# Three feature tiles of a projection abreast on the first chunk of tokens, weights and some last stores on ScalarE's queue, and a planner fed with traced transfer times

## The chip, the cores and the metric

The kernel runs on one core of one Trainium2 chip. Time is the device time of one execution in microseconds (us). Before the change it is 802.28 us, the median of three runs (800.56 to 803.45). A profiled execution gives the trace from which all durations here are read. The engines are PE (TensorE, matmuls; PEld is its weight load), ACT (ScalarE), DVE (VectorE), POOL (GpSimd) and SP (SyncE, which here issues nearly all transfers).

## The reference

Two independent branches over 2048 tokens of 448 features are computed, and their results stand side by side in an output of 2048 x 896.

```python
# A: Fourier mixing, y = Re(DFT_seq(DFT_hidden(x)))
a = einsum("bsd,ed->bse", x, dft_hid_re)
b = einsum("bsd,ed->bse", x, dft_hid_im)
y = einsum("ts,bse->bte", dft_seq_re, a) - einsum("ts,bse->bte", dft_seq_im, b)
# B: softmax attention, 16 heads of 28 features
q, k, v = split(x @ wqkv)
p = softmax(q @ k.T * 28 ** -0.5)
o = (p @ v).reshape(B, S, D) @ wo
# result
concatenate([y, o], axis=-1)
```

## The kernel before

**Products.** Most products are made of rounded high parts and small remainders: x = xh + xl, w = wh + wl, and xh wh + xl wh + xh wl is summed. A contraction over 448 features is three tiles of 128 and one of 64, whose high and low rows share one tile; so one product of a 128 x 512 block takes 11 matmuls: three for each of the first three tiles of features (quarters, below) and two for the last. ACT copies a landed piece into its rounded high part, DVE subtracts to get the low part.

**Stages.** Tokens come in 4 chunks of 512 (`load_x`, four transfers of 256 KB per chunk, one for each quarter of the features). `project` makes q and k of one feature tile of 128 (7 tiles, weights by `Piece`, 256 KB each) for the chunks that it is given; `values` makes v for a chunk, in four tiles of 128 tokens. The results go to DRAM (`qkd`, `vd`). Then the Fourier branch's hidden product (`hidden_both`, L891), its sums over mirrored rows (`combine`) and its sequence product in 4 chunks for each of two parts (`sequence_halved`, L1175) run between the attention of 16 heads: score matmuls (L1434), their exponential on ACT (L1438), and value matmuls (L1445) in groups of 16 tiles. `normal` takes a head's row sums through DRAM and multiplies by their reciprocals; `project_late` multiplies by `wo` (L1676 for the first three quarters of the features, L1707 for the last, which needs the last heads).

**The planner.** Nothing of the order is written out by hand. `Schedule` collects every instruction as a task with its engine, an estimated duration, dependencies, the buffers that it takes and a key, which is the time at which it is due. `run` then plays the kernel through: each free engine takes the ready task with the least key, and that fixes the order of each engine's queue when the kernel is built. On the chip each queue runs in that order and waits where something isn't there. The durations and the transfer times in it are constants: `FLOW_IN` and `FLOW` for the rate of transfers, `FIRST` for when an engine begins, `PE_TURN` for the switch from score to value matmuls, and for each transfer a size and an `extra`. `T_ATT` and `T_END` spread the keys of the 16 heads, `T_FILL` spreads those of all other matmuls (the fill), `T_OUT` is the key of the last stage, and `PV_LATE` puts the key of a group of value matmuls so many steps (one score matmul's share of the time of attention) behind its last score.

**Buffers.** `kept` is a pool of 20 pairs of 128 x 512 values that nearly every stage uses; a group of value matmuls holds 8 of them. `whi` and `wraw` have 3 buffers each, `wlo` has 5. Of the 8 PSUM banks 4 belong to the fill, 4 to attention, which may borrow the fill's.

**The start.** PE runs 11 warm-up pairs on an identity matrix (L1535). SP issues x's first quarter, the weights of feature tile 0, x's other three quarters, then the weights of v. PE runs the 11 matmuls of feature tile 0 for chunk 0, in the order in which their pieces come, then the values of chunk 0, then tile 0 for chunks 1 to 3, then the values of chunks 1 to 3, then the feature tiles 1 to 6 for all four chunks.

**The end.** In `project_late` the first nine matmuls of an output tile run early. Of the 16 tiles, those from 0 to `N_HELD` - 1 are copied out and held in SBUF until the last quarter's two matmuls are added by DVE; the others stay in a fill bank, and the last two matmuls add to it. Each tile is stored by SP (L1712 for held ones, L1716 for the others). After that every engine loads a flag that says whether the shortcuts held (L1746) and branches past a slower way to compute the same (L1747).

Of the kernel before, what the change touches and what calls it, by code (L numbers as in the profile page):

```python
# [22 lines left out]
D = 448  # L23
H = 16
DH = 28
# [18 lines left out]
N_WARM = 11  # L44
GV = 4
# [6 lines left out]
N_HELD = 12  # L52
# [11 lines left out]
NOTE_AT = 7.0  # L64
# [7 lines left out]
PV_LATE = 8.0  # L72
LATE_BOTH = 3.0
LATE_SPREAD = 3.5
LATE_RAW = 1.0
LATE_FIRST = 1.05
LATE_SUMS = 1.1
# [98 lines left out]
class Schedule:  # L176
# [38 lines left out]
    def run(self):  # L215
# [10 lines left out]
        while True:  # L226
            for e in self.ENGINES:
# [115 lines left out]
def tile_kernel(ctx, tc, xa, wre, wim, wd, xb, wqkv, wo, out):  # L343
# [122 lines left out]
    def dma(key, emit, size=256, extra=0.0, n=1, **kw):  # L466

        return sch.add({"SP": 0.4}, key, lambda e: emit(), dmas=[(size, extra)] * n, **kw)
# [22 lines left out]
    T_END = 740.0  # L491
    T_FILL = 950.0
    T_OUT = 806.0
# [74 lines left out]
    def load_x(c, key):  # L568
        cols = slice(c * CH, (c + 1) * CH)
        for k in range(4):  # L570
            pair = kept_s.slot()
            raw = Half(pair, 0)
            ld = dma(key + 0.3 * k, lambda raw=raw, k=k: nc.sync.dma_start(raw.t, xb[c, :, k]), use=[pair])
# [11 lines left out]
    def load_w(w, src, key, after=(), early=False):  # L585
        ts = []
        for k in range(4):
            raw = kept_s.slot() if early else wraw.slot()
            r2 = lambda raw=raw: raw.t.rearrange("p a b -> p (a b)")[:, :D]
            ld = dma(key + 0.3 * k, lambda r2=r2, k=k: nc.sync.dma_start(r2(), src(k)), acq=[raw])  # L590
# [9 lines left out]
    class Piece:  # L600


        def __init__(self, src, key, kind="c", early=False):
            self.hi, self.lo = whi.slot(), wlo.slot()
            raw = wraw.slot()
            ld = dma(key, lambda: nc.sync.dma_start(raw.t, src()), acq=[raw])
# [42 lines left out]
    def project(j, w, chunks):  # L649

        for c in chunks:
# [4 lines left out]
            first = j == 0  # L656
# [10 lines left out]
            else:  # L667
# [6 lines left out]
            end = chain(key, seq, o, CH, [], [w.hi, w.lo], M512, own, parts)  # L674
            key, out_key = (0.0, 11.0) if first else (key - 10, key - 10)
# [5 lines left out]
                dma(out_key, lambda hi=hi, cols=cols: nc.sync.dma_start(f32(qk_d[j * P:(j + 1) * P, 0, cols]), as_f(hi.t)), deps=[a], use=own),  # L681
                dma(out_key, lambda lo=lo, cols=cols: nc.sync.dma_start(f32(qk_d[j * P:(j + 1) * P, 1, cols]), as_f(lo.t)), deps=[b], use=own)]
# [1125 lines left out]
```

## Time and profile before

| | us |
|---|---|
| median of three runs | 802.28 (800.56 to 803.45) |
| the profiled execution's own time | 803.39 |
| span in it, first to last instruction | 801.5 |
| PE / ACT / DVE / POOL busy | 785.5 / 589.1 / 422.1 / 66.4 |
| mean granted clock of TensorE | 0.992 |

In a row of the timeline stand the start, the length, the engine, the line, the operation, the tile written and those read, their shapes and how many instructions were merged; in brackets stands how long the engine was idle before it and what ended that. SPq is the queue of SP: its length there is the time of issue, not of the transfer. In the list of waits the arrow points to what was waited for. In the table of stages each engine has its busy time and, in brackets, its number of instructions. In the chain that ended last, each piece was released by the one ahead of it.

### The profile page before, as it was taken

How to read it: one execution, taken by the hardware profiler on the slowest of the kernel's cores; microseconds unless marked ns; L12 is line 12 of the kernel's file. 1: busy time of each engine (PE TensorE's matmuls, PEld its weight loads, DVE VectorE, ACT ScalarE, POOL GpSimd, SP SyncE). 2: the span in 40 equal slices, each digit the busy share in tenths (PEclk: the TensorE clock that was granted, in tenths of full speed). 3: DMA queues.
4: the chain of work that ended last, by engine and by line, in shares of the span. 5: the costliest groups of instructions: out<-in, count | busy, mean ns of one | idle time of the engine just before them, and what ended most of it. 6: DMA issues, size and time to landing. Idle time of an engine off the chain costs nothing.

```text
span 801.5 us, 14235 instructions
## 1 busy us (share of the span) xinstructions
PE 785.5 (98%) x4721; PEld 476.3 (59%) x4721; DVE 422.1 (53%) x894; ACT 589.1 (74%) x1218; POOL 66.4 (8%) x220
## 2 busy tenths in 40 slices
PE   8999999999999999999999999999999999999995
PEld 7886555665566556555555555565455555555584
DVE  6642234262253456225477665668877766664342
ACT  6106887747878588888888887888788788889831
POOL 3000000000001010100121110111021102100000
PEclk9999999999999999999999999999999999999998
DMA  8857856652467756475678874785787867875143
GB/s 284 250 148 251 228 179 183 196 199 100 129 159 176 220 173 189 140 211 159 192 237 241 270 233 134 232 276 173 184 269 215 249 179 242 255 242 175 27 127 112
DMA packets 148023, 157.09 MB, mean 196 GB/s; under 512 B 39832, under 2 KB 116214, under 8 KB 147942
## 3 DMA queue, kind: packets, MB, share of 16 engines
q1 hardware_dynamic: 144774, 152.41, 63.2%
q0 software_dynamic: 3168, 3.69, 1.6%
q8 instruction: 40, 0.66, 0.4%
q14 instruction: 41, 0.34, 0.1%
HBM read 114.59 MB, written 50.99 MB: 207 GB/s over the span
## 4 chain that ended last, share of the span: by engine, by line
PE 88%; DMA 4%; ACT 3%; DVE 2%; SPq 1%; issue 1%; POOL 0%; DVEq 0%; ACTq 0%; POOLq 0%
PE bank L1434 29%; PE bank L1445 27%; PE bank L636 13%; PE bank L1175 8%; PE bank L891 5%; ACT kept L1438 3%; PE bank L1676 3%; DMA edge<-wim 1%; PE bank L1707 1%; PE bank L1418 1%; DMA xraw<-wim 1%; DMA kept<-xb 1%; DMA wdraw<-wim 1%; DMA kept<-ond 1%; PE bank L1094 0%
## 5 line engine op out<-in xcount | busy, mean ns | idle before, releaser
L1438 ACT ACTIVATE kept<-bank 128x512 f32<-128x512 f32 x1024 | 509.7, 676 | 111.3 <-PE bank L1434 102.7
L1434 PE MATMUL bank<-q,k 85*128 85x512 f32 x1024 | 362.3, 424 | 0.3 <-DVE kept L1273 0.3
L1434 PEld LDWEIGHTS bank<-q,k 85*128 85x128 f32 x1024 | 184.6, 190 | 87.9 <-issue 33.1
L1445 PE MATMUL bank<-kept,v 128*32 128x512 f32 x2048 | 234.3, 598 | 0.0
L1445 PEld LDWEIGHTS bank<-kept,v 128*32 128x32 f32 x2048 | 60.2, 110 | 133.7 <-issue 130.4
L1175 PE MATMUL bank<-zt 128*128 128x226 bf16 x448 | 78.1, 266 | 1.2 <-DVE zt L1218 1.2
L487 DVE COPY kept<-bank 128x448 f32<-128x448 f32 (+3 forms) x66 | 32.1, 508 | 84.6 <-PE bank L891 52.4
L636 PE MATMUL bank<-xt,whi 128*128 128x512 f32 x196 | 70.1, 402 | 1.5 <-DVE xt L481 1.3
L1131 DVE TENSOR_REDUCE diff<-zt 128x1 f32<-128x512 bf16 x77 | 51.6, 679 | 2.2 <-POOL zt L1228 0.7
L1175 PEld LDWEIGHTS <-zt 128*128 128x128 bf16 x448 | 30.6, 99 | 35.4 <-issue 25.9
L636 PEld LDWEIGHTS bank<-xt,whi 128*128 128x128 f32 x196 | 36.7, 191 | 13.1 <-issue 2.5
L636 PE MATMUL bank<-xt,wlo 128*128 128x512 f32 x112 | 44.0, 394 | 0.0
L891 PE MATMUL bank<-wd,whi 128*128 128x450 f32 (+3 forms) x128 | 42.1, 379 | 0.0
L1175 PE MATMUL bank<-xt,whi 128*128 128x448 f32 (+1 forms) x128 | 40.1, 339 | 1.1 <-DVE kept L1273 1.1
L636 PE MATMUL bank<-wd,xt 128*128 128x448 f32 x176 | 37.1, 368 | 0.0
L636 PEld LDWEIGHTS bank<-wd,xt 128*128 128x128 f32 x176 | 32.8, 188 | 3.5 <-issue 0.7
L1218 DVE TENSOR_TENSOR zt<-wdraw,xraw 128x508 bf16<-128x508 f32 x28 | 19.1, 682 | 25.4 <-PE bank L1175 10.6
L1129 ACT ACTIVATE spent<-zt 128x512 uint8<-128x512 bf16 x35 | 25.1, 716 | 5.3 <-DVE zt L1209 3.0
L1421 DVE STREAM_TRANSPOSE kept<-bank 128x512 f32<-128x512 f32 (+1 forms) x20 | 14.2, 712 | 27.2 <-PE bank L1418 27.2
L1175 PEld LDWEIGHTS bank<-xt,whi 128*128 128x128 f32 x128 | 25.0, 201 | 5.7 <-ACT kept L1438 1.7
L487 DVE CAST wd<-bank 128x512 fp32r<-128x512 f32 x8 | 5.5, 690 | 43.2 <-PE bank L636 43.2
L1498 ACT ACTIVATE kept<-bank 128x512 f32<-128x512 f32 (+1 forms) x19 | 11.3, 595 | 22.9 <-PE bank L1445 21.3
(172 smaller groups left out, 722.4 us busy)
## 6 DMA issues: line engine op xcount, KB each, us to landing
wdraw<-wim SPq DMA_DIRECT2D x38, 256.0 KB
qkd<-wd SPq DMA_DIRECT2D x32, 256.0 KB
wdraw<-wre SPq DMA_DIRECT2D x32, 256.0 KB
q<-qkd SPq DMA_DIRECT2D x64, 112.0 KB
k<-qkd SPq DMA_DIRECT2D x64, 112.0 KB
abd<-kept SPq DMA_DIRECT2D x16, 448.0 KB
kept<-abd SPq DMA_DIRECT2D x16, 448.0 KB
qkd<-kept SPq DMA_DIRECT2D x24, 256.0 KB
```

What stands on the lines that cost most here:

```text
L487: nc.vector.tensor_copy(dst, src)
L636: nc.tensor.matmul(o.t[:, :cols], w(), x(), start=(i == 0), stop=(i == n - 1))
L891: nc.tensor.matmul(o.t[:, c0:c1], of(w, i), y(), start=n == 0, stop=n == m)
L1129: nc.scalar.activation(spent, src(), AF.Abs, accum_out=dst)
L1131: nc.vector.tensor_reduce(dst, src(), axis=AX.X, op=ALU.add, apply_absolute_value=True)
L1175: nc.tensor.matmul(o.t[:, at0:at0 + n], cut_of(w.t, e, c), x(), start=first, stop=stop)
L1218: e.tensor_tensor(turned(dl.t, 1, 1, P - 1), mirror(r.t), read(base.t, 1, 1, P - 1), op=minus)
L1421: r = dve(key, lambda o=o, mt=mt: nc.vector.transpose(mt.t[:32 * n, 0], o.t[:32 * n]), 0.64, deps=[m], acq=[mt], use=[o], own=RAW_S)
L1434: m = pe(key, lambda e: nc.tensor.matmul(b.t, KT[h][kt // 4].t[:KR + 1, kt % 4 * P:(kt % 4 + 1) * P], q.t[:KR + 1, :], start=True, stop=True),
L1438: return act(key - 20, lambda: nc.scalar.activation(p.t, b.t, AF.Exp, scale=SCALE), deps=[m], use=[b, pair])
L1445: nc.tensor.matmul(o.t[j * VW:(j + 1) * VW, :], VT[h].t[:, kt // 4, kt % 4, :], tiles[i // 2].t[:, i % 2, :], start=(kt < 4 // len(cs)), s ...
L1676: nc.tensor.matmul(o.t[:, :D], a(), b(), start=(i == 0), stop=(i == 8 and n < N_HELD))
```

## The change

Chunk 0 is projected for feature tiles 0, 1 and 2 before its values are made. The weights of these three tiles are issued by ScalarE's queue ahead of its own work, the chains of tiles 1 and 2 are not tied to the chain of tile 0, and each of their matmuls depends only on its own piece of x and w. Later the loop over tiles gives tiles 1 and 2 only chunks 1 to 3. There are 9 warm-up pairs instead of 11 and 10 held output tiles instead of 12. Of the tiles that are not held, those of odd number are stored by ScalarE's queue. All other edits are numbers of the planner: transfers get an issue time (`each`) and another `extra`, and the rates, the turn, the due times and `PV_LATE` change. `VALUES` replaces `GV` with the same groups of four.

```diff
-N_WARM = 11
-GV = 4
+N_WARM = 9
+EARLY = 3
+VALUES = (4, 4, 4, 4)
...
-N_HELD = 12
+N_HELD = 10
...
-NOTE_AT = 7.0
+NOTE_AT = 9.0
...
-PV_LATE = 8.0
-LATE_BOTH = 3.0
...
+PV_LATE = 11.0
...
-FLOW, FLOW_IN = 250.0, 400.0
+FLOW, FLOW_IN = 250.0, 260.0
...
-FIRST = {"PE": 1.4, "ACT": 2.0, "DVE": 2.0, "POOL": 5.0, "SP": 0.75}
-FLOW_AT = 4.1
+FIRST = {"PE": 1.4, "ACT": 0.75, "DVE": 2.0, "POOL": 5.0, "SP": 0.75}
+FLOW_AT = 2.4
...
-PE_TURN = 0.22
-GAP = 0.6
+PE_TURN = 0.33
+GAP = 0.3
 JOIN = 15.0
-LAG = 60.0
+LAG = 100.0
...
-                    for size, extra in t.dmas:
+                    for size, extra, each in t.dmas:
...
-                        landed.append(max(at + 1.9 + size / 100 + extra + (3.0 if T_IN - 6 < now < 42 else 0.0), flow + 1.1))
-                        at += 0.38
+                        landed.append(max(at + 1.9 + size / (100 if now > T_IN - 6 else 140) + extra + (3.0 if T_IN - 6 < now < 42 else 0.0), flow + 1.1))
+                        at += each
...
+    def dma_act(key, emit, lat, **kw):
+
+        return sch.add({"ACT": 0.42}, key, lambda e: emit(), lat=lat, own=lat, **kw)
...
-    T_END = 740.0
-    T_FILL = 950.0
-    T_OUT = 806.0
+    T_END = 720.0
+    T_FILL = 930.0
+    T_OUT = 815.0
...
-            ld = dma(key, lambda: nc.sync.dma_start(raw.t, src()), acq=[raw])
+            if early:
+                ld = dma_act(key - 5, lambda: nc.scalar.dma_start(raw.t, src()), 4.6, acq=[raw])
+            else:
+                ld = dma(key, lambda: nc.sync.dma_start(raw.t, src()), each=0.66, acq=[raw])
...
-    def project(j, w, chunks):
+    def project(j, w, chunks, last=last):
...
-            first = j == 0
+            first = j == 0 or j < EARLY and c == 0
...
-            end = chain(key, seq, o, CH, [], [w.hi, w.lo], M512, own, parts)
-            key, out_key = (0.0, 11.0) if first else (key - 10, key - 10)
+            end = chain(key, seq, o, CH, [], [w.hi, w.lo], M512, own, parts, last)
+            key, out_key = (0.0, 11.0 + j) if first else (key - 10, key - 10)
...
-        return Piece(lambda: wqkv[:, :, j * P:(j + 1) * P], 0.2 if j == 0 else key, "w", j == 0)
+        return Piece(lambda: wqkv[:, :, j * P:(j + 1) * P], 0.2 + 0.25 * j if j < EARLY else key, "w", j < EARLY)
...
-        return pe(key, emit, d=0.22 * len(kts) * len(cs), deps=[*es, *got_v[h], after], use=[*tiles, VT[h], o], mode=1)
+        return pe(key, emit, d=0.2133 * len(kts) * len(cs), deps=[*es, *got_v[h], after], use=[*tiles, VT[h], o], mode=1)
...
-        s2 = dma(key, lambda: nc.sync.dma_start(sm.t[:, :n * NC], osb.t[DH:n * VW:VW, :]), 8, 3.0, deps=[a], use=[sm, pair])
+        s2 = dma(key, lambda: nc.sync.dma_start(sm.t[:, :n * NC], osb.t[DH:n * VW:VW, :]), 8, 0.6, each=0.67, deps=[a], use=[sm, pair])
...
-    w_0 = weights_of(0)
+    w_early = [weights_of(j) for j in range(EARLY)]
...
-    project(0, w_0, [0])
+    for j in range(EARLY):
+        project(j, w_early[j], [0], last if j == 0 else [None])
     values(wv, [0])
-    project(0, w_0, [1, 2, 3])
+    project(0, w_early[0], [1, 2, 3])
     values(wv, [1, 2, 3])
     x_users.append(v_last[0])
     for j in range(1, 7):
-        project(j, weights_of(j), range(NC))
+        project(j, *((w_early[j], range(1, NC)) if j < EARLY else (weights_of(j), range(NC))))
...
-                dma(key, lambda pair=pair, n=n: nc.sync.dma_start(out[n * P:(n + 1) * P, D:], pair.t[:, 0, :D]), deps=[e], use=[pair])
+                if n % 2:
+                    dma_act(key, lambda pair=pair, n=n: nc.scalar.dma_start(out[n * P:(n + 1) * P, D:], pair.t[:, 0, :D]), 3.0, deps=[e], use=[pair])
+                else:
+                    dma(key, lambda pair=pair, n=n: nc.sync.dma_start(out[n * P:(n + 1) * P, D:], pair.t[:, 0, :D]), deps=[e], use=[pair])
```

More of the change, by code (lines that the diff above doesn't have):

```diff
@@ L939, in put @@
                                   rows_at(src, (P - p) * row if p else P, [[P * row, HT], [-row, r], [1, FT * P]]))
-            base_turned[part, n] = dma(key + n * step, put, 256 if n else 16, extra=4.0, hold=True)
+            base_turned[part, n] = dma(key + n * step, put, 256 if n else 16, extra=1.5, each=0.75, hold=True)
     def turn_rows():
@@ L1063, in put @@
                 nc.sync.dma_start(x.t[:65:32, 1, CH - 1:], rows_at(src, HT * P * row + FT * P, [[0, 3], [1, 1]]))
-        ld = dma(key, put, 12, n=3 - part, extra=6.0, deps=[*zs, ab_done[FT], ab_done[HT + FT], *after], use=[w, x])
+        ld = dma(key, put, 12, n=3 - part, extra=6.0, each=0.9, deps=[*zs, ab_done[FT], ab_done[HT + FT], *after], use=[w, x])
         wide = lambda p0=0: w.t.rearrange("p a b -> p (a b)")[p0:96, part::2]
@@ L1469, in head_once @@
             got_q.append([*load_q((h, c), q, at - 14), dma(
[L1470 removed]
+                at - 11, lambda q=q, row=row: nc.sync.dma_start(f32(q.t)[KR:KR + 1, :], row), size=2, extra=0.4, each=0.3, deps=[s], use=[q])])
             qs.append(q)
@@ L1485, in head_once @@
                 es.append(score(h, c, kt, qs[c], got_q[c], tiles[-1], i % 2, key))
-            last_pv = four(h, po, tiles, es, key + PV_LATE * DT, range(GV * g, GV * (g + 1)), range(NC), last_pv)
+            last_pv = four(h, po, tiles, es, key + PV_LATE * DT, range(first, first + n), range(NC), last_pv)
+            first += n
         normal([(h, c) for c in range(NC)], h, po, last_pv, key + 10)
```

74 lines of the change are left out of this document (35 added, 39 removed).

## The prediction

> **What bounds the kernel now.** I read the page's head and busy shares first, then the slices with the chain of waits, then PE's waits, and last a table of stages and the timelines of both ends.
>
> ```profile
> span 801.5 us, 14235 instructions
> PE 785.5 (98%) x4721; PEld 476.3 (59%) x4721; DVE 422.1 (53%) x894; ACT 589.1 (74%) x1218; POOL 66.4 (8%) x220
> PE   8999999999999999999999999999999999999995
> PEclk9999999999999999999999999999999999999998
> PE 88%; DMA 4%; ACT 3%; DVE 2%; SPq 1%; issue 1%; POOL 0%; DVEq 0%; ACTq 0%; POOLq 0%
> ```
>
> TensorE (PE) is busy 785.5 of 801.5 us, only the first and last slices are not full, and 88% of the chain that ends last is PE's. So only 16.0 us can be won without taking work from PE. The list of PE's waits and the stages say where they lie:
>
> ```profile
> PE bank L1418 <- ACT kept L1438: 1.5, 1, 1.5
> PE bank L1535 <- POOL ident masks.py:199: 1.4, 1, 1.4
> PE bank L636 <- DVE xt L481: 1.3, 1, 1.3
> PE bank L1175 <- DVE zt L1218: 1.2, 2, 0.8
> PE bank L1175 <- DVE kept L1273: 1.1, 1, 1.1
> PE bank L1707 <- DVE q L1697: 0.8, 1, 0.8
> ...
> 5.00:10.00 5.00, 4.30 (x16) 3.20 (x15) 2.89 (x6) 2.81 (x6) 1.52 (x15) 1.00 0.94 303
> 10.00:15.00 5.00, 4.40 (x21) 3.98 (x22) 4.88 (x9) 4.73 (x9) 1.24 (x12) 1.00 1.03 375
> 20.00:25.00 5.00, 5.00 (x24) 4.13 (x23) 4.88 (x11) 2.30 (x4) 0.00 (x0) 1.00 1.07 303
> 790.00:801.50 11.50, 2.47 (x11) 1.62 (x10) 1.94 (x3) 1.69 (x3) 0.00 (x0) 0.76 0.25 87
> ```
>
> A wait's columns are its total, how often, and the longest. Those of a stage its length, then PE, weight loads, DVE, ACT and POOL busy, the granted clock, the DMA share and GB/s. The last stage alone has 9.0 us without matmuls (11.50 - 2.47). The longest wait in the middle is 1.5 us; three (1.5, 1.2 and 1.1) make 3.8 us. So three places can change: the start, the end, and the order in between.
>
> **The start.** This is the first chunk of tokens before the change; the last row gives the pitch of a 512-column matmul.
>
> ```profile
> 0.76 1.28 ACT L575 ACT_TABLE_LOAD   x1 [0.76 <-PEq L1801]
> 0.76 0.39 SPq L573 DMA_DIRECT2D kept<-xb  x1
> 1.21 0.69 SPq L606 DMA_DIRECT2D wraw<-wqkv  x1
> 1.38 5.07 PE L1535 MATMUL bank<-ident 128*128 128x128 f32 x22 [1.38 <-POOL ident masks.py:199]
> 4.49 0.63 ACT L575 ACTIVATE xt<-kept 128x512 fp32r<-128x512 f32 x1 [2.44 <-DMA kept<-xb]
> 5.32 0.63 ACT L607 ACTIVATE whi<-wraw 128x512 fp32r<-128x512 f32 x1 [0.20 <-DMA wraw<-wqkv]
> 5.98 0.56 DVE L611 TENSOR_TENSOR wlo<-wraw,whi 128x384 fp32r<-128x384 f32 x1
> 6.10 1.62 PE L636 MATMUL bank<-xt,whi 128*128 128x512 f32 x3
> 6.46 0.28 DVE L620 TENSOR_TENSOR wlo<-wraw,whi 64x128 fp32r<-64x128 f32 x1
> 9.20 0.63 ACT L575 ACTIVATE xt<-kept 128x512 fp32r<-128x512 f32 x1 [1.18 <-DMA kept<-xb]
> 9.86 0.69 DVE L481 TENSOR_TENSOR xt<-kept,xt 64x512 fp32r<-64x512 f32 x1 [1.12 <-ACT xt L575]
> 11.18 0.77 PE L636 MATMUL bank<-wd,xt 128*128 128x448 f32 x3
> 60.43 7.75 PE bank L636 x34
> ```
>
> A matmul of 512 columns takes 7.75 / 34 = 0.228 us. The 11 of the first chain need 2.51 us, but from the first (6.10) to the start of the values (11.18) pass 5.08: 2.57 us are lost, because each quarter of x comes only as fast as its transfer, the last at 9.20. The change puts 22 more matmuls into these holes (feature tiles 1 and 2 of the same tokens, 5.02 us, taken out of later places). Before, the same 33 and their holes count as 11.18 + 5.02 = 16.20 on this clock. With no hole and the same start they end at 6.10 + 33 x 0.228 = 13.62: a gain of at most 2.6 us. It can't be had in full:
>
> - Two more weights must come, 256 KB each. At 303 GB/s (stage 5 to 10) 512 KB are 1.7 us of transfer. If all of it comes ahead of x, the first matmul is at 7.8 and the 33 end at 15.3: gain 0.9 us. If only the last quarter of x is late (10.9), it has its 0.63 on ACT and 0.69 on DVE by 12.3, the six matmuls that need it (1.37 us) end at 13.7, and almost nothing is lost.
> - ACT makes three weights instead of one, 7 x 0.63 = 4.4 us with x, from 4.49 on: done by 8.9 if nothing waits, and the last x comes later anyway. The three issues stand ahead of the table load, which carries the line of the first activation (L575); at 0.69 each (SP's row) they and the 1.28 us load end by 0.76 + 2.07 + 1.28 = 4.11, before the first x at 4.49. This cover is thin: were the load first, the first weight would be issued at 2.04 instead of 1.21 and all would start 0.8 us later.
> - DVE makes two more low halves (0.56 + 0.28 each, 1.7 us) in 5 to 10, where it is busy 2.89 of 5 us. From 10 on it has no room (4.88 of 5), but there it also gets these 1.7 us back, since the same work stood there later.
> - SP's queue loses the weight ahead of x's second quarter (0.69 us) and so issues x sooner. The four stores of the extra tiles (256 KB each) move to 11 to 16 us, between loads of later x, as key 11 + j puts them; PE needs that x 3 us later than before, which covers them.
> - Two warm-up pairs fewer (5.07 / 11 = 0.46 us each) end the warm-up at 5.5 instead of 6.45; matmuls wait for data at 6.1, so I cost this at nothing.
>
> I take **-1.7 us**, midway between 0.9 and 2.6; the bounds for the range are 0 (loads crowded and table load first, 0.9 - 0.8) and -2.6.
>
> The Trainium skill's page "DMA: Bandwidth & Descriptors", section "Issuing engines are not separate DMA queues", speaks against part of this: transfers issued from different engines share the same 16 DMA engines and interleave, and a second issuer saves only issue time. The stage 10 to 15 agrees as far as it goes (DMA share 1.03). By that rule the two weights are paid for in full, the start gives 0.9 instead of 1.7 us, and the sum is 798.8.
>
> **The end.**
>
> ```profile
> 780.00:790.00 10.00, 10.00 (x51) 9.28 (x50) 2.90 (x5) 1.06 (x3) 0.00 (x0) 1.00 0.38 125
> 780.29 1.78 PE L1707 MATMUL bank<-wout,q 128*128 128x448 f32 x8
> 791.38 1.88 PE L1707 MATMUL bank<-wout,q 128*128 128x448 f32 x8 [0.79 <-DVE q L1697]
> 792.66 2.90 SPq L1716 DMA_DIRECT2D out<-kept  x4
> 792.90 0.55 ACT L485 ACTIVATE kept<-bank 128x448 f32<-128x448 f32 x1 [0.27 <-PE bank L1707]
> 793.30 0.62 DVE L487 COPY kept<-bank 128x448 f32<-128x448 f32 x1 [0.18 <-PE bank L1707]
> ...
> L1746 SPq TENSOR_LOAD <-flag x1: 609/609/609, 795.6 to 795.6; - x1
> L1747 SPq COMPARE_BRANCH  x1: 50/50/50, 796.6 to 796.6; - x1
> SPq L1747 <- SPq L1747: 2.6, 1, 2.6
> L1747 DVEq EVENT_SEMAPHORE  x1: 21/21/21, 797.8 to 797.8; - x1
> ```
>
> The last copy is done at 793.92, but SP issues the four last stores one behind another until 795.56, then loads the flag, branches at 796.6, waits 2.6 us and only then (799.2) runs out to 801.5. DVE, which branched earlier, was through at 797.8. After the change tiles 13 and 15 (and 11, by `n % 2` from tile 10 on) go by ScalarE's queue. SP's last store then waits only for ACT's copy (793.45), takes some 0.5 us and ends near 794.0 instead of 795.56. ACT's last store starts at 793.92 and ends near 794.4. With the same way to the end behind it SP is through at 797.7, about where DVE is. So up to 1.6 us go; I take **-1.4 us**, bounds -1.7 and 0 (the landing of the last store, not the branch, would then set the end). On ACT a store waits for DVE's copy, and behind it stand only the next tile's copy and the flag: at worst one DVE copy, 0.6 us, included in the bound.
>
> With 10 held tiles, 6 stay in the four fill banks; tiles 14 and 15 can begin their 9 matmuls only when tiles 10 and 11 have left. Of the 51 matmuls between 780 and 790 (0.196 us each), 8 belong to chunk 2's rest; the other 43, or 8.4 us, are such work that had not run by then, more than the 18 x 0.196 = 3.5 us of tiles 14 and 15, so the wait for a bank is covered. If chunk 2's rest came less than 3.5 us before the fill ends, the difference would be lost; two additions on DVE go, off the path.
>
> **The order in between.** All other edits alter no instruction of the kernel but the planner's costs, due times and transfer times, so each queue's order changes over 800 us. Attention's due times close 20 us sooner (740 to 720) and the fill's too (950 to 930). The fill's due times run evenly from about 52 to 950, so (950 - 740) / 898 = 23.4% of it is due behind attention before and (930 - 720) / 878 = 23.9% after. That half per cent of the fill, itself less than half of PE's 785.5 us, is at most 2 us more cover for the last head's chain, where PE waited 0.8 us. No transfer stands among PE's waits, so truer landings have little to win; new order shifts the 3.8 us of middle waits about. Bounds: all 3.8 and the 0.8 gone, or as much again, +4.6. I take a quarter of the gain, **-1.2 us**, as nothing in the diff addresses those buffers by itself.
>
> **Sum.** The profiled execution took 803.39 us (span 801.5 and 1.9 around it): 803.4 - 1.7 - 1.4 - 1.2 = 799.1. It lies 1.1 above the median of 802.28, so I forecast 798.0 for a median.
>
> **Rivals** (0.3%, 2.4 us, is about what a measurement of this kernel can tell from no change: 799.9 and 804.7).
>
> 1. **The order loses too (slower).** The third edit of weight is that value groups come due 11 steps late instead of 8. A step is (740 - 35) / 1024 = 0.69 us before and 0.67 after, so a group's 8 buffer pairs of 20 are held 7.4 instead of 5.5 us. Where two groups and a sum's three buffers are wanted at once the pool is dry, and PE's fill waits for DVE's freeing as at L1273, 1.1 us. Against it: this wait came once in 801 us. It decides if it comes at all eight chunks of the sequence stage: + 8 x 1.1 - 1.7 - 1.4 = +5.7, about 808. Five such waits, +2.4, already make it slower. Chance 0.11.
> 2. **The loads are crowded, the end is held by landings (no change).** Start -0.9 by the sum above, end -0.3, middle 0: 801.1. For it: DMA share 1.03 in 10 to 15; against it: the last x quarter, not the first, is what PE waits longest for. Chance 0.25. (By the Trainium skill's rule above, the start goes this way.)
> 3. **The new order also removes the middle's waits.** -2.6 - 1.6 - 4.6 = -8.8 from the start's and end's bounds: about 793.5. Chance 0.14.
> 4. **It doesn't do what it says:** the extra chains stand in PE's fixed order where their weights aren't there yet, so PE waits as before in other places. Start 0, end -1.4, middle 0: 800.9. Part of "no change", within rival 2's chance.
>
> The forecast itself (796 to 799.9) has 0.50. Range 793.0 to 804.0: from rival 3 to the upper side of no change; left out are rival 1 and a little below. Faster 0.64 (forecast and rival 3), same 0.25, slower 0.11.
>
> **What would show it.** Start: three weight loads issued on ACT before 2.9 us, the table load behind them, 33 matmuls with x and whi or wlo before the first with wd, and that one near 14.5 (16.2 would be no gain). End: the span ends about 6 us after the last copy instead of 7.6, with SP's last store ending within 0.5 us of it. Middle: no wait in PE's list over 1.5 us. The forecast is wrong if the first matmul with x comes after 7.0, if a wait of PE on DVE's kept stands three times or more, or if the last group of matmuls waits over 2 us for its q.

## The result, and the profile after

The change makes the kernel slower: **805.48 us** (median of 22 runs, 802.05 to 810.48) against 801.55 us (22 runs, 796.73 to 806.83), ratio 1.0054 with a 95% interval of [1.0032, 1.0076]. The forecast was 798.0, with a range of 793.0 to 804.0. The profiled execution took 807.78 us.

The page of the kernel after, first its head and slices:

```profile
span 805.9 us, 14248 instructions
PE 790.5 (98%) x4717; PEld 476.8 (59%) x4717; DVE 424.0 (53%) x900; ACT 582.7 (72%) x1199; POOL 69.8 (9%) x220
PE   7999999999999999999999999999999999999997
PEclk9999999999999998999999999999989999999999
```

PE is busy 5.0 us longer (790.5 for 785.5) at the same work. Two slices of the granted clock show an 8 in the middle, where the kernel before has none. PE's waits after:

```profile
PE bank L1437 <- DVE kept L487: 3.4, 2, 2.1
PE bank L639 <- ACT whi L610: 3.3, 2, 2.9
PE bank L1540 <- POOL ident masks.py:199: 1.4, 1, 1.4
PE bank L1437 <- DMA q<-md: 0.7, 1, 0.7
```

With one of 0.2 us these are all, 9.0 us in sum where the list of before had 7.8. That doesn't make 4 us. The time shows in the table of stages, by its granted clock (the column ahead of the last two):

```profile
7.90:11.31 3.41, 2.99 (x6) 1.66 (x6) 2.31 (x6) 1.78 (x5) 0.00 (x0) 0.50 1.06 357
300.00:304.90 4.90, 2.81 (x14) 2.06 (x13) 2.04 (x6) 4.06 (x9) 0.53 (x2) 1.00 0.71 204
304.90:311.70 6.80, 6.80 (x28) 2.87 (x30) 1.49 (x4) 2.75 (x6) 0.00 (x0) 0.50 0.51 154
582.10:588.20 6.10, 6.10 (x16) 2.41 (x13) 5.93 (x15) 6.10 (x14) 0.00 (x0) 1.00 0.68 54
588.20:595.00 6.80, 6.80 (x28) 2.06 (x31) 6.58 (x16) 3.07 (x7) 0.94 (x4) 0.50 0.78 219
```

The same table for the kernel before:

```profile
270.41:273.82 3.41, 3.41 (x18) 1.03 (x22) 1.62 (x3) 0.35 (x1) 0.00 (x0) 0.50 0.46 99
604.91:608.32 3.41, 3.41 (x13) 2.73 (x12) 3.41 (x7) 2.42 (x5) 0.35 (x2) 0.50 0.68 235
796.06:801.50 5.44, 0.00 (x0) 0.00 (x0) 0.00 (x0) 0.00 (x0) 0.00 (x0) 0.50 0.19 62
```

For 3.4 or 6.8 us at a time TensorE was granted **half its clock** (0.50). Such stretches stand at 7.9, 270.7, 304.9 and 588.2 us, 20.5 us in all; the kernel before has two of 3.4 us, at 270.4 and 604.9. Each follows a stretch in which PE had little to do. At the end, where no matmul is left, both have one more (5.4 us before, 2.7 after), which costs nothing. The third row of the kernel after shows PE as busy 6.80 of 6.80 us, so "busy" doesn't tell. The matmuls' own rows do:

```profile
303.90 0.73 PE L1437 MATMUL bank<-q,k 85*128 85x512 f32 x2 [2.09 <-DVE kept L487]
...
582.11 8.05 PE L1437 MATMUL bank<-q,k 85*128 85x512 f32 x16
590.09 6.05 PE L1448 MATMUL bank<-kept,v 128*32 128x512 f32 x32
...
605.99 3.64 PE L1448 MATMUL bank<-kept,v 128*32 128x512 f32 x32
```

A group of 32 value matmuls takes 6.05 us in the stretch and 3.64 outside it: 2.4 us lost in that one row. Ahead of it stand 16 scores in a row with no fill between them. They took 0.50 us each (8.05 / 16), ScalarE's pace for their exponentials, where a 512-column matmul takes 0.228: TensorE had work for under half of those 8 us, though the page counts it busy throughout.

I split the span of both profiles by the starts of the matmuls. What exceeds a matmul's time at full clock, up to the next one's start, is put down to a half-clock stretch, to a gap of over 0.43 us, or to a smaller gap:

| us | before | after | difference |
|---|---|---|---|
| start (first value matmul, less 0.228 for each x matmul ahead of it) | 8.7 | 10.2 | +1.5 |
| matmuls at full clock | 712.3 | 712.3 | 0 |
| lost in half-clock stretches | 3.1 | 9.2 | +6.1 |
| gaps over 0.43 us | 6.2 | 4.6 | -1.6 |
| smaller gaps | 62.6 | 63.3 | +0.7 |
| from the last matmul's start to the end | 8.6 | 6.3 | -2.3 |
| span | 801.5 | 805.9 | +4.4 |

The rows of half clock and gaps depend on the price of a matmul; another price moves their differences by up to 0.7 us.

The start after, and below it the end:

```profile
0.76 2.00 ACTq L607 DMA_DIRECT2D wraw<-wqkv  x3
1.38 3.74 PE L1540 MATMUL bank<-ident 128*128 128x128 f32 x18 [1.38 <-POOL ident masks.py:199]
2.80 1.28 ACT L575 ACT_TABLE_LOAD   x1 [2.80 <-issue]
4.57 0.63 ACT L575 ACTIVATE xt<-kept 128x512 fp32r<-128x512 f32 x1 [0.49 <-DMA kept<-xb]
6.84 0.63 ACT L575 ACTIVATE xt<-kept 128x512 fp32r<-128x512 f32 x1 [1.64 <-DMA kept<-xb]
7.37 0.61 ACT L610 ACTIVATE whi<-wraw 128x512 fp32r<-128x512 f32 x1
8.04 2.56 PE L639 MATMUL bank<-xt,whi 128*128 128x512 f32 x5 [2.92 <-ACT whi L610]
17.72 1.58 PE L639 MATMUL bank<-wd,xt 128*128 128x448 f32 x7
...
799.40 0.57 PE L1713 MATMUL bank<-wout,q 128*128 128x448 f32 x2
800.01 0.54 ACT L485 ACTIVATE kept<-bank 128x448 f32<-128x448 f32 x1 [1.69 <-PE bank L1713]
800.58 0.34 ACTq L1723 DMA_DIRECT2D out<-kept  x1
```

On ACT the second quarter of x (6.84) stands ahead of the first weight (7.37); before, the weight came first (5.32). By the trace the first weight landed at 6.20, before at 5.29. So the first matmul starts at 8.04 instead of 6.10, some 0.9 us of it by the later landing and some 1.2 by ACT's order. It comes after 2.92 us without work, and at half clock: the first five take 0.51 us each (2.56 / 5). At the end the span runs 5.4 us past the last copy (800.55) instead of 7.6.

### The profile page after: what moved, and what is told of

It is laid out like the page before. It is cut to its first block, busy times and chain, and to the rows that moved or that the text cites. A ratio compares the mean times of both kernels' runs of the same rounds, so it can differ in the third digit from the quotient of the medians.

```text
span 805.9 us, 14248 instructions
## 1 busy us (share of the span) xinstructions
PE 790.5 (98%) x4717; PEld 476.8 (59%) x4717; DVE 424.0 (53%) x900; ACT 582.7 (72%) x1199; POOL 69.8 (9%) x220
## 4 chain that ended last, share of the span: by engine, by line
PE 91%; DMA 5%; ACT 2%; SPq 1%; DVE 1%; issue 0%; ACTq 0%; DVEq 0%
PE bank L1437 30%; PE bank L1448 28%; PE bank L639 13%; PE bank L1178 9%; PE bank L894 4%; PE bank L1682 4%; ACT kept L1441 1%; DMA wraw<-wqkv 1%; DMA sm<-kept 1%; PE bank L1421 1%; PE bank L1713 1%; DMA kept<-rd 1%; DMA xraw<-wre 1%; PE bank L1097 0%; DMA q<-qkd 0%
## 5 line engine op out<-in xcount | busy, mean ns | idle before, releaser
L1437 PE MATMUL bank<-q,k 85*128 85x512 f32 x1024 | 366.7, 424 | 4.2 <-DVE kept L487 3.4
L1448 PE MATMUL bank<-kept,v 128*32 128x512 f32 x2048 | 239.1, 608 | 0.0
L487 DVE COPY kept<-bank 128x226 f32<-128x226 f32 (+3 forms) x61 | 29.2, 498 | 96.6 <-PE bank L894 50.0
L1134 DVE TENSOR_REDUCE diff<-zt 128x1 f32<-128x512 bf16 x88 | 57.7, 679 | 2.8 <-POOL zt L1231 1.9
L894 PE MATMUL bank<-wd,whi 128*128 128x450 f32 (+3 forms) x128 | 43.9, 382 | 0.2 <-DVE kept L487 0.2
L485 ACT ACTIVATE kept<-bank 128x448 f32<-128x448 f32 (+2 forms) x20 | 11.8, 605 | 24.8 <-PE bank L639 11.8
L894 PEld LDWEIGHTS bank<-wd,whi 128*128 128x128 f32 (+1 forms) x128 | 23.5, 192 | 5.6 <-ACT kept L1441 2.5
L1227 POOL TENSOR_TENSOR zt<-wdraw,xraw 128x2 bf16<-128x2 f32 x28 | 11.0, 393 | 163.6 <-PE bank L1178 54.8
```

What stands on the lines that cost most here:

```text
L485: nc.scalar.activation(dst, src, AF.Copy)
L487: nc.vector.tensor_copy(dst, src)
L894: nc.tensor.matmul(o.t[:, c0:c1], of(w, i), y(), start=n == 0, stop=n == m)
L1134: nc.vector.tensor_reduce(dst, src(), axis=AX.X, op=ALU.add, apply_absolute_value=True)
L1437: m = pe(key, lambda e: nc.tensor.matmul(b.t, KT[h][kt // 4].t[:KR + 1, kt % 4 * P:(kt % 4 + 1) * P], q.t[:KR + 1, :], start=True, stop=True),
L1448: nc.tensor.matmul(o.t[j * VW:(j + 1) * VW, :], VT[h].t[:, kt // 4, kt % 4, :], tiles[i // 2].t[:, i % 2, :], start=(kt < 4 // len(cs)), s ...
```

## The experiments

All ratios are to the kernel before on the same chip. The last column is worked out from the mean granted clock of the runs: t us at half clock lower the mean over 800 us by t / 1600. It counts the end, too, where no matmul runs: 5.4 us of it in the profile before, 2.7 in the one after. So on matmuls it is, by estimate, some 3 us before and 15 after. It leaves out the first microseconds, for which the trace has no clock.

| kernel | median us | ratio [95% interval] | us at half clock |
|---|---|---|---|
| before (123 runs) | 800.86 | | 8.6 |
| after | 805.48 | 1.0054 [1.0032, 1.0076] | 18.1 |
| e1_numbers | 803.58 | 1.0041 [1.0012, 1.0070] | 16.0 |
| e2_stores | 801.68 | 1.0019 [0.9997, 1.0041] | 8.8 |
| e3_abreast | 810.69 | 1.0138 [1.0092, 1.0184] | 22.4 |
| e4_warm | 803.85 | 1.0022 [0.9991, 1.0052] | 14.3 |
| e5_landings | 812.61 | 1.0148 [1.0119, 1.0177] | 23.2 |
| e6_cold | 798.59 | 0.9963 [0.9931, 0.9995] | 6.1 |
| e7_held10 | 797.43 | 0.9961 [0.9928, 0.9994] | 6.4 |
| e8_twice | 805.69 | 1.0054 [1.0022, 1.0087] | 12.9 |
| e9_nosums | 805.08 | 1.0045 [1.0017, 1.0074] | 17.5 |
| e10_by_sp | 806.07 | 1.0071 [1.0040, 1.0101] | 21.1 |
| e11_turn | 800.04 | 0.9987 [0.9962, 1.0012] | 7.8 |
| e12_end | 800.71 | 1.0002 [0.9979, 1.0024] | 6.9 |
| e13_pv8 | 805.61 | 1.0058 [1.0034, 1.0082] | 9.3 |
| e14_pv8_warm | 807.00 | 1.0076 [1.0040, 1.0111] | 8.8 |
| e15_held_cold | 799.00 | 0.9978 [0.9947, 1.0009] | 6.0 |
| e16_note9 | 803.01 | 1.0030 [1.0005, 1.0054] | 11.1 |

### Which part of the change

**e1_numbers** keeps the planner's numbers of the change and undoes the rest.

```diff
-EARLY = 3
+EARLY = 1
-N_WARM = 9
+N_WARM = 11
-N_HELD = 10
+N_HELD = 12
```

(ACT's first time, the issue of the weights and the stores are as before, too.)

> The changed kernel with the start and the end of the kernel before (one early tile, its weights and all last stores by SP, 11 warm-up pairs, 12 held tiles); the planner's numbers stay those of the change. Theory A (the new landings put the head's reciprocal and multiplication into DVE's queue too early; DVE waits, banks come free late, PE stalls and the half clock follows): DVE waits 20 us or more for sm and 10 or more for rd, as after (26.1 and 14.0), and the time stays 1 to 4 us above before. Theory B (the start alone makes it slower): the loss of 1.5 us at the start is gone and the time is that of before within 1 us.

It was slower, 1.0041, with 16.0 us at half clock, and it has the run of scores too: 16 of them from 577.8 to 585.7 us, with half clock from 582.0 to 588.8. The planner's numbers alone bring a loss nearly as large as that of the whole change.

**e2_stores** is the kernel before with the odd last tiles stored by ScalarE's queue.

```diff
-                dma(key, lambda pair=pair, n=n: nc.sync.dma_start(out[n * P:(n + 1) * P, D:], pair.t[:, 0, :D]), deps=[e], use=[pair])
+                if n % 2:
+                    dma_act(key, lambda pair=pair, n=n: nc.scalar.dma_start(out[n * P:(n + 1) * P, D:], pair.t[:, 0, :D]), 3.0, deps=[e], use=[pair])
+                else:
+                    dma(key, lambda pair=pair, n=n: nc.sync.dma_start(out[n * P:(n + 1) * P, D:], pair.t[:, 0, :D]), deps=[e], use=[pair])
```

> The kernel before with the last stores of odd tiles moved to ScalarE's queue, nothing else. If the end's mechanism is right: from the end of the last copy to the end of the span some 5.4 us as after, instead of 7.6, and the time 1.4 to 2.2 us below before. If the landing of the last store sets the end: within 0.5 us of before.

No gain. Its end, in the timeline and in the waits of SP's queue:

```profile
793.79 1.89 SPq L1723 DMA_DIRECT2D out<-kept  x2
794.03 0.54 ACT L489 ACTIVATE kept<-bank 128x448 f32<-128x448 f32 x1 [0.27 <-PE bank L1711]
794.28 1.40 ACTq L1721 DMA_DIRECT2D out<-kept  x2
...
SPq L1754 <- SPq L1754: 3.6, 1, 3.6
```

Two stores on each queue are issued in 1.89 and 1.40 us, but SP then waits 3.6 us at the branch instead of 2.6, and the span ends 7.4 us after the last copy instead of 7.6. What SP saves in issue it spends at the branch.

**e3_abreast** is the kernel before with the three tiles abreast and their weights by ScalarE's queue, and nothing else but ACT's first time.

```diff
+EARLY = 3
...
-FIRST = {"PE": 1.4, "ACT": 2.0, "DVE": 2.0, "POOL": 5.0, "SP": 0.75}
+FIRST = {"PE": 1.4, "ACT": 0.75, "DVE": 2.0, "POOL": 5.0, "SP": 0.75}
...
-    project(0, w_0, [0])
+    for j in range(EARLY):
+        project(j, w_early[j], [0], last if j == 0 else [None])
```

> The kernel before with the three feature tiles abreast and their weights by ScalarE's queue, with before's planner numbers (ACT's begin aside). Theory B: first matmul with x near 8.0, the values begin at 17.2 or later where 16.2 would be even, and the time is 1 to 2 us above before. Theory A: DVE's waits for sm and rd stay near 8.7 and 4.9 us, and what is lost is the start alone, 1 to 2 us; a time of 803 to 806 would speak against A.

Slower by 1.4%, some 10 us where 1 to 2 were expected. The first matmul came at 7.50 us, earlier than after, with ACT converting the first weight (landed 6.27) ahead of x. The values began at 16.06, about level with 16.2, so the loss isn't at the start: a new order with five stretches of half clock followed. Abreast without the planner's new numbers is worse than with them.

**e10_by_sp** gives the three weights of the kernel after back to SP's queue, in turn with x.

```diff
-                ld = dma_act(key - 5, lambda: nc.scalar.dma_start(raw.t, src()), 4.6, acq=[raw])
+                ld = dma_act(key - 5, lambda: nc.sync.dma_start(raw.t, src()), 4.6, acq=[raw])
```

> The changed kernel with the three early weights issued by SP in the same plan (in turn with the quarters of x), everything else in the same order. If ScalarE's queue makes the first weight late (its 512-byte rows take turns with x's 2 KB rows): the first matmul with x at 6.0 to 6.8 instead of 8.0, the values at 15.5 to 16.5 instead of 17.7, no half clock at the start, and the time 1.5 to 3 us below 805.5. If the bytes alone set it: the first matmul at 7.3 or later and the values at 17 or later.

```profile
5.80 0.63 ACT L575 ACTIVATE xt<-kept 128x512 fp32r<-128x512 f32 x1 [3.76 <-DMA kept<-xb]
8.23 0.63 ACT L575 ACTIVATE xt<-kept 128x512 fp32r<-128x512 f32 x1 [1.80 <-DMA kept<-xb]
8.77 1.13 ACT L610 ACTIVATE whi<-wraw 128x512 fp32r<-128x512 f32 x2
...
9.44 2.08 PE L639 MATMUL bank<-xt,whi 128*128 128x512 f32 x4 [3.94 <-ACT whi L610]
```

The first weight was issued first of all and by the trace landed at 4.16, and still waited behind x's second quarter (landed 8.21) in ACT's fixed order: the first matmul came later (9.44). So with the weight early, ACT's order sets the first matmul. Giving the issue back to SP made x later, and the kernel didn't become faster.

### Is it DVE's waits for landings?

In the kernel after DVE waits far longer for two transfers of `normal` (the row sums and their reciprocals): 40.1 us, where before it was 13.6. The list of DVE's waits:

```profile
DVE sm L1508 <- DMA sm<-kept: 26.1, 9, 6.9
DVE kept L1519 <- DMA kept<-rd: 14.0, 6, 4.8
```

**e5_landings** gives the planner later landings for these two.

```diff
-        s2 = dma(key, lambda: nc.sync.dma_start(sm.t[:, :n * NC], osb.t[DH:n * VW:VW, :]), 8, 0.6, each=0.67, deps=[a], use=[sm, pair])
+        s2 = dma(key, lambda: nc.sync.dma_start(sm.t[:, :n * NC], osb.t[DH:n * VW:VW, :]), 8, 3.0, each=0.67, deps=[a], use=[sm, pair])
...
-        s4 = dma(key, spread, 64, 2.0, n=n, deps=[s3], use=[pair])
+        s4 = dma(key, spread, 64, 3.5, n=n, deps=[s3], use=[pair])
```

> The changed kernel with two landings set back to the numbers of before (row sums 0.6 to 3.0, the spread reciprocals 2.0 to 3.5), nothing else. Theory A: DVE's waits for sm and rd fall from 40.1 us together to under 20, no wait of PE over 1.2 us in the middle, and the time is 2 to 4 us below the changed kernel's 805.5. Theory B: no change within 1 us, since the start is the same.

```profile
DVE kept L1519 <- DMA kept<-rd: 5.7, 3, 2.1
DVE sm L1508 <- DMA sm<-kept: 4.1, 1, 4.1
```

The waits fell from 40.1 to 9.8 us and the kernel became 7 us slower than after, with 23.2 us at half clock; its order is a new one, too. **e9_nosums** takes the reciprocal and the check of the sums out of the kernel after and adds instead of multiplying, so its result is another.

```diff
-        r = dve(key - 20, lambda: nc.vector.reciprocal(sm.t[:, :n * NC], sm.t[:, :n * NC]), 0.3, deps=[s2], use=[sm])
+        r = dve(key - 20, lambda: None, 0.3, deps=[s2], use=[sm])
...
-        mul = dve_on(key - 20, lambda e: e.tensor_tensor(osb.t[:n * VW], osb.t[:n * VW], sbc.t[:n * VW], op=ALU.mult), 0.62,
+        mul = dve_on(key - 20, lambda e: e.tensor_tensor(osb.t[:n * VW], osb.t[:n * VW], sbc.t[:n * VW], op=ALU.add), 0.62,
```

> The changed kernel without the two small DVE instructions behind the row sums' landing (the reciprocal and its maximum), which leaves out the division by the row sums, and with an addition in place of the multiplication by them, of the same size; the planner still counts both, so every other order is kept. If DVE standing before a late landing is what stops PE near 301 us: DVE's 26 us of waits for sm are gone, so are PE's 2.1 us wait for DVE kept L487 and the half clock from 304.9, and the time falls by 2 to 4 us below the changed kernel's 805.5. If the half clocks have other causes: the same half clock per run and the same time within 1.5 us.

DVE's waits for the sums are gone, and the time is the same (805.08). But 26.3 us of waits for the transfer behind them remained (14.0 after), and so did a wait of PE for DVE's kept L487 (3.3 us). After these two runs my first theory, that DVE's waits for landings are where the time went, had nothing left to speak for it; disproved it isn't, since neither run took the waits alone away.

### Is it the half clock?

**e4_warm** is the kernel after with 15 warming pairs emitted for 9, in an unchanged order.

```diff
-        for _ in range(N_WARM):
+        for _ in range(N_WARM + 6):
```

> The changed kernel with 15 warm-up pairs emitted instead of 9, all else in the same order: the warm-up now lasts to about 7.8 and fills the hole before the first matmul with x at 8.0. Theory C (half clock follows a window in which PE did little): the half clock at 7.9 to 11.3 is gone, the six first matmuls take 1.4 instead of 3.0 us, the values begin at 16.2 to 16.8 instead of 17.7, and the time falls by about 1.2 us. Theory D (the half clock comes by chance, the weights' landing sets the start): half clock near 8 as before, values at 17.7, no change.

```profile
1.38 5.35 PE L1540 MATMUL bank<-ident 128*128 128x128 f32 x30 [1.38 <-POOL ident masks.py:199]
7.52 0.96 PE L639 MATMUL bank<-xt,whi 128*128 128x512 f32 x3 [0.79 <-ACT whi L610]
```

PE idles 0.79 us instead of 2.92, the first matmuls take 0.32 us each instead of 0.51, the stretch at the start is gone, the values begin at 16.98 instead of 17.72, and the median is 1.6 us lower, though the intervals of the two ratios overlap. **e6_cold** is the reverse: the kernel before with 4 pairs for 11.

```diff
-        for _ in range(N_WARM):
+        for _ in range(N_WARM - 7):
```

> The kernel before with 4 warm-up pairs emitted instead of 11, all else in the same order: PE idles from about 3.1 to 6.1. Theory C: a half clock of 3.4 us or more begins between 5 and 9, the values begin up to 1.5 us later than 11.2, and the time rises by 0 to 1.5 us. Theory D: no half clock in the first 15 us and the same start.

```profile
1.38 2.07 PE L1535 MATMUL bank<-ident 128*128 128x128 f32 x8 [1.38 <-POOL ident masks.py:199]
5.86 1.22 PE L636 MATMUL bank<-xt,whi 128*128 128x512 f32 x2 [2.41 <-ACT whi L607]
...
8.73 1.05 PE L636 MATMUL bank<-xt,whi 128*128 128x512 f32 x2
9.58 0.63 PE L636 MATMUL bank<-xt,wlo 128*128 128x512 f32 x1
```

The table of stages shows 1.00 here, but the trace's record of the clock begins only at 12.45 us in this run (7.58 before, 4.49 after), and what isn't recorded counts as full. Ahead of it the matmuls run at half clock: from 8.73 to 9.58 two take 0.43 us each. In the kernel after, a warm-up matmul takes 0.213 us ahead of the record's begin and 0.110 behind it. So with 4 warm-up pairs half clock lasted to 12.45 us. It mostly hid behind x's transfers: the values begin at 11.39 instead of 11.18. The time went down to 0.9963, where theory C had 0 to 1.5 us more.

The Trainium skill's page "TensorE: Matmul & The Clock Gate", Part 1, says that the clock halves after a free-running window of some 3.4 us in which TensorE idles. The steps of 3.41 us agree: in each of the twenty profiles the clock changes only at whole steps, on a grid of its own. But a step needn't be idle. I estimated how much of each step at full clock the matmuls in it would fill at full speed (0.228 us for 512 columns). All 30 steps filled under 0.40 were followed by half clock, 22 of the 58 filled from 0.40 to 0.60, and none of the 4490 filled more. So a gap counts by how much of one step it empties, and scores at ScalarE's pace (0.46) can do the same without a gap; what decides between 0.40 and 0.60 stays open.

**e16_note9** sets one planner's number in the kernel before, which puts 13 scores in a row where it had none.

```diff
-NOTE_AT = 7.0
+NOTE_AT = 9.0
```

> The kernel before with NOTE_AT 9 for 7, one number of the change. Its planned order has a run of 13 scores at the place where the kernel after has 16 and the kernel before has none. Theory of the half clock: TensorE falls to ScalarE's pace there, the granted clock is halved near 585 us for 3.4 to 6.8 us, and the time rises by 1 to 3 us, to 802 to 804 us. Rival (a run of scores alone costs nothing): same time as before within 0.3%.

The timeline and the stages at that place:

```profile
567.05 6.54 PE L1434 MATMUL bank<-q,k 85*128 85x512 f32 x13
573.51 5.60 PE L1445 MATMUL bank<-kept,v 128*32 128x512 f32 x32
...
567.00:570.70 3.70, 3.70 (x11) 1.52 (x9) 3.60 (x9) 3.70 (x9) 0.00 (x0) 1.00 0.69 75
570.70:577.50 6.80, 6.80 (x26) 2.43 (x29) 6.58 (x16) 3.52 (x8) 0.00 (x0) 0.50 0.69 137
```

As forecast, though at 570.7 us and not near 585: 13 scores at 0.50 us, 3.7 us into them the clock halves for 6.8 us, and the values behind take 5.60 us. The time is 0.30% longer, with an interval from 0.05 to 0.54%; the rival's bound was 0.3%. So this is one way in which a planner's number brings half clock, and by the median it costs 2 us.

**e8_twice** makes the 16 scores of the kernel after twice (the second result is the same as the first), to keep PE busy through that run.

```diff
+            for _ in range(2 if FROM <= made[0] - 1 < TO else 1):
+                nc.tensor.matmul(b.t, KT[h][kt // 4].t[:KR + 1, kt % 4 * P:(kt % 4 + 1) * P], q.t[:KR + 1, :], start=True, stop=True)
```

> The changed kernel with 16 score matmuls, those issued from 580.9 to 589.5 us, each made twice in a row (the second overwrites the first with the same numbers); order kept, 16 matmuls more. There PE runs at the pace of ACT's exponentials, one score of 0.23 us each 0.49 us. Theory C: with this stretch streamed full, the half clock of 6.8 us from 588.2 is gone or at most 3.4 us, the value matmuls behind it take 3.6 instead of 6.05 us, and the time falls by 2 to 4 us although there is more work. Theory D: half clock as before, time the same or up to 3.6 us longer.

The half clock behind the run went (5.2 us less of it in a run), and the time stayed (805.69). The 16 extra matmuls cost up to 16 x 0.228 = 3.6 us if none is hidden, so this run tells of the clock and not of the time. **e13_pv8** parts the same scores without extra work, by one number of the change put back.

```diff
-PV_LATE = 11.0
+PV_LATE = 8.0
```

> The kernel after with one planner's number put back: the values' order number PV_LATE 8 for 11. In the planned order the 16 scores in a row of 582 to 590 us are parted, everything that the start and the landings do stays. Theory of the half clock (time is about 797 us plus 0.49 us for each us at half clock): the stretch at 588 to 595 us goes, some 3 to 5 us less at half clock in an execution, and the time falls 1.5 to 2.5 us, to 803 to 804 us. Rival (the number acts by its order alone, the clock is a bystander): the time stays at 805.5 or moves without the mean clock. If another run of scores or another wait takes its place, the half clock shows at that place.

```profile
589.78 3.64 PE L1448 MATMUL bank<-kept,v 128*32 128x512 f32 x32
...
588.00:595.00 7.00, 7.00 (x48) 3.17 (x48) 6.87 (x14) 5.49 (x13) 1.45 (x5) 1.00 0.82 251
```

The run of scores and its half clock are gone, the mean over 12 runs fell from 18.1 to 9.3 us at half clock, **and the time did not move**: 805.61. That isn't quite the level of the kernel before: in the profile only 0.7 of the 7.5 us at half clock are at the end, and 6.8 stand at the start. **e14_pv8_warm** adds e4's edit.

> The kernel after with PV_LATE 8 and 15 warming pairs for 9, which keeps TensorE busy up to about 7 us. Theory of the half clock: the stretches at 8 us and at 588 us are both gone, the mean granted clock comes near that of the kernel before (0.9947), and the time is 801 to 802.5 us, so that the change with its start, its stores and all its landings is level with the kernel before. Rival: the order made for the new landings loses by itself, and the time stays at 804 us or more.

Again 8.8 us at half clock and no gain, 807.00. For both my theory named 801 to 804, and the rival was right. Both profiles came from executions at the lower end of their runs. **e17_pv8_look** (808.38 us) and **e18_warm_look** (808.02 us) are one more profiled execution of each kernel.

> The kernel of e13_pv8 once more, one look, for a second profiled execution. If its time is in waits of TensorE that hardly lower the clock, the profile shows 3 to 5 us more in stalls or in small gaps between matmuls than the kernel before, at a mean clock of 0.994 or higher. If half clock does all of it, an execution near 806 us shows a mean clock below 0.990.

> The kernel of e14_pv8_warm once more, one look. The same reading as for e17_pv8_look: 3 to 5 us more in stalls and small gaps at a clock of 0.994 or higher, or a clock below 0.990. The start should again have no half clock, with values near 17 us.

The start of e17_pv8_look's values, the stages around its second stretch, and the longest wait of e18_warm_look:

```profile
19.70 1.58 PE L639 MATMUL bank<-wd,xt 128*128 128x448 f32 x7
...
608.00:610.30 2.30, 0.91 (x4) 0.59 (x4) 2.23 (x6) 1.83 (x4) 0.56 (x3) 1.00 0.67 179
610.30:617.10 6.80, 6.56 (x26) 3.58 (x30) 6.80 (x17) 3.11 (x6) 1.63 (x4) 0.50 0.86 272
```

```profile
PE bank L1421 <- DMA qb<-qkd: 2.6, 1, 2.6
```

Other waits (1.6 us before 610.5, and 2.6 before 129.0) brought half clock at places that the first execution of the same kernel had without; there the first wait was absent and the second 0.74 us. The mean clocks, 0.990 and 0.993, lie between what the two forecasts named. Split as above, e17 stands to the kernel before at start +3.5, half clock +0.3, gaps over 0.43 us +1.7, smaller gaps +2.2, end -2.5; e18 at +0.9, +1.9, +1.4, +3.0 and -2.4. So with the planned run gone, the loss stands in gaps between matmuls, spread over the kernel (+3.9 and +4.4), and in e17 as much in the start, where the half clock lasts 6.8 us.

**e11_turn** and **e12_end** move one number of the kernel before a little (`PE_TURN` 0.22 to 0.23, `T_END` 740 to 738).

> The kernel before with one planner number moved by a little (PE_TURN 0.22 to 0.23), which changes nothing but the order. If the order of before is as good as its neighbours': within 1.5 us of before, half clock 9 us per run as there. If any new order costs (as the planner's numbers alone did, 2.4 us): 2 us or more above before, with more half clock.

> The kernel before with one planner number moved by a little (T_END 740 to 738), which changes nothing but the order. As for PE_TURN: within 1.5 us of before if its order is like its neighbours', 2 us or more above before with more half clock if any new order costs.

Neither differs from the kernel before. As far as two neighbours show it, its order is not a lucky one, and the loss is not what any new order brings.

### A version that beats both

**e7_held10** is the kernel before with one number changed.

```diff
-N_HELD = 12
+N_HELD = 10
```

> The kernel before with 10 held output tiles instead of 12, all stores by SP; the order of PE is the same up to the last 40 us. If the 10 held tiles shorten the end: 6.4 us or less from the end of the last copy to the end of the span (before 7.6, after 5.4), one tile instead of four behind the last x quarter, and 1 to 2 us less time. If the last matmul only comes later by what the end gains: the time of before within 0.5 us.

Its 797.43 us is the lowest median of all, 0.9961 [0.9928, 0.9994], under the kernel before and the one after. But the end hardly moved: 7.35 us from the last copy to the end of the span, where 6.4 or less was expected and before has 7.61. In its profile no half clock falls on matmuls. **e15_held_cold** joins it with e6's edit.

> The kernel before with 10 held tiles for 12 and 4 warming pairs for 11, each of which alone gave 0.996 of the time before. If the gains are of separate places (the end, and waits that gave half clock in the middle) they add up to 0.992 to 0.994, 795 to 796.5 us; if both are only other draws of the same chance at half clock, the two together are again 797 to 799 us with a mean clock near 0.996.

The two gains don't add up (0.9978, an interval that reaches 1.0009). Two of seventeen kernels with an interval just below 1 are weak evidence, and I would take e7's edit, which costs nothing, without counting on its 0.4%.

## Why the prediction was wrong

**The order in between is the step that failed.** The prediction gave it -1.2 us, with bounds of 4.6 us either way; by the split it is +5.2 (6.1 - 1.6 + 0.7). The sign named for it, no wait of PE over 1.5 us, failed with 2.1. I had counted only waits, "the 3.8 us of middle waits". In that currency the change even gained 1.6 us. What it lost is the speed of TensorE behind them: a wait of 2 us, or 8 us at ScalarE's pace that no list of waits shows, is followed by up to 6.8 us at half clock. Before, the same happened behind the 1.5 us wait, and the page's clock row, all nines but the last, hid it in slices of 20 us. Over the 316 executions of all kernels, compared within each kernel, a microsecond at half clock goes with 0.52 us of time (correlation 0.82). The 9.5 us more of it after the change come to 4.9 us (some 6 without the end, where it costs nothing), more than the whole difference; that is an association, and e16 shows one case of it made on purpose. e13 and e14 show its limit: with half of the half clock gone the time stayed. So the order that the new numbers make costs some 4 us, whether they stand as half clock or as gaps; e1, with the old start, points to the same size. Which of its placements is to blame, beyond `NOTE_AT` (e16, +0.3%), stays open.

**The start** was to give -1.7 us, at worst 0; it is +1.5 in this execution, and that is a mild one. Of five more profiles with the same start e8 has +1.7, and e5, e9, e13 and e17 have +3.3 to +3.7: their half clock lasts 6.8 us there, and the values begin at 19.50 to 19.86. The forecast had 14.5, and 16.2 as no gain. The other points named for it came true (weights issued before 2.9, the table load behind them, 33 matmuls ahead of the values), and so did the condition under which the forecast is wrong, a first matmul after 7.0. Two terms failed. With the transfers abreast the first weight landed 0.9 us later (5.29 to 6.20), where the working took a value midway between no delay and a crowded start. And I summed ACT's seven conversions and took their order to be that of arrival; ACT's queue is fixed when the kernel is built, and x's second quarter stood ahead of the first weight, some 1.2 us (e10 shows the same with an early weight). The two warm-up pairs fewer, "at nothing", then let the idle time reach 2.92 us, and its half clock takes 0.7 us of the start here (e4: 17.72 to 16.98) and more where it lasts 6.8. The working had also put the whole 2.57 us lost before down to x's transfers, though its three first matmuls, 0.54 us each, ran at half clock.

**The end** was to give -1.4 us and gives -2.3, but not by its mechanism: stores on ScalarE's queue alone gained nothing (e2). In the profile after, the last tile's one copy and one store end the work, while PE is full until 800 us. From the last matmul's start to the end it is 8.6 before, 7.2 in e1 with its stores on SP, 6.3 after: over half of it is the planner's order. What the stores and the held tiles do together beyond that wasn't tried alone.

**The rivals.** Rival 1 had the right sign and nearly the size (808), but not the mechanism: PE waited twice on DVE's `kept`, not eight times. Rival 2 was right that the start is crowded. Nowhere in the working stands the clock, though the quoted last stage has a 0.76.

## What to carry to other kernels

Price a wait of TensorE by what follows it: look for a granted clock of 0.5 in stages of 3 to 7 us, and for runs of matmuls that take twice their time at a full "busy", before calling a stage full. At the start, read the clock from the matmuls' own times, since the trace may not record it yet. When a planner's constants are changed, treat the whole new order as the change and run it alone first; truer constants didn't make a better order here. A conversion that must come first has to be first in its engine's fixed queue, since an early transfer doesn't move it.

## What the runs showed of the hardware

The granted clock falls for 3.4 or 6.8 us, in two kernels for 10.2 (e5 and e9), behind gaps of 1.1 us (before, ahead of 604.9) to 2.9 us (after, ahead of 8.04), and behind scores that fill TensorE to 46% (0.228 of 0.50 us). It follows steps of 3.41 us that are filled too little: always under 0.40, never over 0.60 in these twenty profiles. TensorE also begins at half clock, in e6 up to 12.45 us. Which waits come, and how long they are, differs between executions of one kernel (0.74 us in e14 and 2.65 in e18 at one place), and with it the time: the executions of one kernel lie 3 to 12 us apart.
